# Expert layers of a decay-attention, cosine-MLP and mixture-of-experts kernel: token groups innermost under each half of an expert, and the second layer as seven block products of 256 columns

## The chip, the cores and the metric

The kernel runs on one core of one Trainium2 chip. The metric is the device time of one execution in microseconds (us), lower is better. The engines are TensorE (PE in the rows; PEld is its weight load), VectorE (DVE), ScalarE (ACT), GpSimd (POOL), and SyncE (SP), which issues the transfers.

## What is computed

Three parts follow each other; the output of one is the input of the next.

```python
attn = softmax(causal(scale * q @ k.T + decay(f))) @ v     # 4 x 8 heads, 576 positions, 64 wide
x = attn as [2304 tokens, 512]
h = x @ w_in;  x = (h * cos(h)) @ w_out                     # 512 -> 2048 -> 512
P = exp(x @ w_gate - max); 8 rounds: rows /= their sum, columns /= their sum, *= 2304 / 8
for e in range(8):                                          # the experts: F = 1024
    out += P[:, e:e+1] * (max(x @ w1[e], 0) @ w2[e])        # w1[e] is 512 x 1024, w2[e] 1024 x 512
```

The change lies in the last loop, the experts.

## The kernel before, in words

All matrix products of the experts run in pairs of 16-bit numbers: each fp32 operand is split into a high f16 part (`hi`) and the rest, again in f16 (`lo`), and each product is three passes of TensorE (`PASSES`: hi·hi, hi·lo, lo·hi) that add up in PSUM. Both operands are brought to a common power of two first (`scales`, found by `find_scale` from the largest magnitudes), and `gate` undoes it.

The 2304 tokens are three groups `p` of 768 (two halves of 384), and each expert's F is cut into two halves `hb` of 512. I call the work for one group, one expert and one half of F a **stretch**; there are 3 x 8 x 2 = 48 of them. Before, the loop order is group, expert, half (`blocks`), so the weights of each of the 16 (expert, half) pairs are loaded and prepared three times. Preparing one pair means, per stretch: four transfers of 512 KB into `sg` (`load_raw`, L992), scaling on ACT (`w_scale`, L1045), sums of blocks on POOL for w1 alone (`w1_sums`, L1015, tiles `tm`), the high part on ACT (`w_hi`, L1054) and the low part on POOL in pieces of 256 columns (`w_lo`, L1063, loads the next raw tile at its end).

The **first layer** of a stretch is done in two sets (`m`) of 256 F columns each. A set is a 2 x 2 block product in Winograd's form: seven products of TensorE (`PRODUCTS`, six matmuls of 384 columns each, L1214) instead of eight. Its right-hand operands are seven combinations of the token blocks (`XCS`, tiles `xc`), its left-hand ones seven combinations of weight blocks (`W1T`, tiles `wa`). The seven results are put together by ACT copies (`ct`, L1242) and DVE adds (L1247), then relu and split into the four blocks `h` (`relu_split`, L1231: high part on ACT, low part on DVE). The **second layer** (`second_layer`, L1284) is a plain product: for each of 6 token tiles, 2 sets x 2 z x 3 passes = 12 matmuls of 512 columns (L1291), 72 in a stretch; `leave` (L1302) then adds a token tile, times its gate, into the SBUF accumulator `acc` on DVE (L1320).

Each engine takes its instructions in the order in which the code issues them; nothing reorders them. `hook()` is called after each product and runs the steps of the gate (`sinkhorn`) that are due at that count; `plan` sets after which token tile of the second layer the next stretch's weights are prepared. The seven `xc` tiles of group 0 are made on POOL before the first stretch (`combine_first`, L1083), and those of groups 1 and 2 on DVE and ACT in the last two experts of the group ahead (`combine_sums`, `combine_split`). Just before the experts the MLP part ends (`layer2`, L813, matmuls L822; its results are added into `acc` by DVE, L837).

## Time and profile before

| | |
|---|---|
| time, median of 3 runs | 2078.04 us (2077.55 to 2078.23) |
| profiled execution, first to last instruction (span) | 2075.6 us |
| PE busy | 2049.3 us, 99% of the span |
| ACT, POOL, DVE busy | 1336.1, 1277.9, 1156.3 us (64, 62, 56%) |
| experts, first matmul to last DVE add | 663.13 to 2072.02 us |

How to read it: the profile is of one execution. Its own time is not listed apart from the span; the 2.4 us by which the median of the runs is above the span are what lies around the first and the last instruction. An engine is busy while it computes; matmuls are pipelined, so the mean duration of one matmul in a row (its latency) is longer than its share of the busy time. About two thirds of the span are the experts.

### The profile page before, as it was taken

To read this page: it belongs to the slowest core of one execution; us is meant where nothing else is said; L and a number is where in the kernel's file an instruction comes from. 1 tells how busy PE (TensorE), PEld (TensorE's weight loads), DVE (VectorE), ACT (ScalarE), POOL (GpSimd) and SP (SyncE) were. 2 spreads that over 40 slices of the span, in tenths; PEclk is the share of its full clock that TensorE was granted. 3 is DMA by queue.
4 is the path that set the end of the run, shared out by engine and by line. 5 is a ranking of instruction groups with operands and counts; after the bars stand their busy time and mean duration, and the time that the engine had idled before them with its cause. 6 is when DMAs were issued, how large, how long until landed. Compare 5 with 4: busy or idle time off the path is not lost.

```text
span 2075.6 us, 34054 instructions
## 1 busy us (share of the span) xinstructions
PE 2049.3 (99%) x12461; PEld 1295.1 (62%) x12461; DVE 1156.3 (56%) x2250; ACT 1336.1 (64%) x2479; POOL 1277.9 (62%) x1794
## 2 busy tenths in 40 slices
PE   8999999999999999999999999999999999999999
PEld 6888988898977555555555555555555555555554
DVE  8999788685666654344455444444455444444443
ACT  7888787767654666666566655666566655666553
POOL 7777455151337666766677666766677666766673
PEclk9999999999999999999999999999999999999999
DMA  5454255454301122221222222222222222221221
GB/s 128 101 114 96 71 167 179 127 167 125 109 1 62 51 72 82 72 68 64 82 82 77 87 72 82 73 68 64 82 81 77 87 72 82 72 67 65 82 81 31
DMA packets 176919, 177.52 MB, mean 86 GB/s; under 512 B 64752, under 2 KB 131696, under 8 KB 176752
## 3 DMA queue, kind: packets, MB, share of 16 engines
q1 hardware_dynamic: 176752, 175.35, 27.9%
q8 instruction: 98, 1.61, 0.3%
q14 instruction: 69, 0.57, 0.1%
HBM read 165.54 MB, written 4.87 MB: 82 GB/s over the span
## 4 chain that ended last, share of the span: by engine, by line
PE 91%; DVE 5%; ACT 2%; issue 1%; POOL 1%; DMA 0%; SPq 0%; POOLq 0%; DVEq 0%; ACTq 0%
PE a L1291 36%; PE y L1214 18%; PE bq L1214 13%; PE ph L175 7%; PE a L822 7%; PE pv L593 2%; PE pst L543 2%; PE pss L486 1%; PE pss L487 1%; PE pv L573 1%; PE psq L366 1%; DVE acc L837 1%; POOL w L136 1%; DVE dx L125 1%; DVE t L196 1%
## 5 line engine op out<-in xcount | busy, mean ns | idle before, releaser
L1291 PE MATMUL a<-wb,h 128*128 128x512 f16 x3456 | 754.9, 379 | 0.2 <-ACT acc L1309 0.2
L1291 PEld LDWEIGHTS <-h 128*128 128x128 f16 x3456 | 338.1, 98 | 401.5 <-issue 0.5
L1214 PEld LDWEIGHTS <-wa 128*128 128x128 f16 x4032 | 394.2, 98 | 266.4 <-ACT ct L1242 0.8
L1214 PE MATMUL y<-xc,wa 128*128 128x384 f16 x2304 | 429.5, 326 | 0.1
L1320 DVE SCALAR_TENSOR_TENSOR acc<-a,gate,acc 128x512 f32<-128x512 f32 x264 | 197.3, 749 | 387.9 <-PE a L1291 387.4
L1022 POOL TENSOR_TENSOR tm<-sg 128x256 f32<-128x256 f32 x96 | 71.3, 743 | 447.7 <-issue 429.9
L1214 PE MATMUL bq<-xc,wa 128*128 128x384 f16 x1728 | 327.9, 326 | 0.4 <-ACT ct L1242 0.4
L1242 ACT ACTIVATE ct<-y 128x384 f32<-128x384 f32 x192 | 94.3, 491 | 274.4 <-PE y L1214 274.3
L1072 POOL TENSOR_TENSOR wa<-tm,wa 128x256 f16<-128x256 f32 x384 | 250.3, 686 | 0.0
L1072 POOL TENSOR_TENSOR wb<-sg,wb 128x256 f16<-128x256 f32 x384 | 244.1, 684 | 0.0
L1233 ACT ACTIVATE h<-bq 128x384 f16<-128x384 f32 x288 | 140.8, 489 | 152.3 <-DVE bq L1247 152.1
L1234 DVE SCALAR_TENSOR_TENSOR h<-bq,h 128x384 f16<-128x384 f32 x288 | 159.5, 554 | 127.0 <-ACT h L1233 117.4
L822 PE MATMUL a<-H,w 128*128 128x512 f32 (+1 forms) x960 | 212.6, 369 | 4.9 <-DVE acc L837 2.9
L175 PE MATMUL ph<-xt,w 128*128 128x512 f32 (+1 forms) x960 | 211.5, 369 | 0.0
L1052 ACT ACTIVATE sg<-sg,sw 128x1024 f32<-128x1024 f32 x188 | 209.9, 1142 | 0.0
L822 PEld LDWEIGHTS a<-H,w 128*128 128x128 f32 x960 | 174.4, 188 | 30.3 <-issue 2.5
L1072 POOL TENSOR_TENSOR wa<-sg,wa 128x256 f16<-128x256 f32 x288 | 189.5, 687 | 0.0
L175 PEld LDWEIGHTS ph<-xt,w 128*128 128x128 f32 x960 | 174.9, 188 | 22.8
L1247 DVE SCALAR_TENSOR_TENSOR bq<-bq,ct 128x384 f32<-128x384 f32 x192 | 108.7, 566 | 108.8 <-PE bq L1214 105.1
L1061 ACT CAST wa<-tm 128x1024 f16<-128x1024 f32 x94 | 98.2, 1045 | 97.2 <-POOL tm L1025 97.2
L128 POOL TENSOR_SCALAR w<-dx 128x512 fp32r<-128x512 f32 x32 | 19.8, 620 | 153.9 <-DVE dx L127 149.3
L1061 ACT CAST wb<-sg 128x512 f16<-128x512 f32 x188 | 107.0, 616 | 3.0
(209 smaller groups left out, 2659.4 us busy)
## 6 DMA issues: line engine op xcount, KB each, us to landing
sg<-in_moe_w_dram SPq DMA_DIRECT2D x192, 512.0 KB
seen<-in_moe_w_dram SPq DMA_DIRECT2D x64, 256.0 KB
u<-in_moe_w_dram SPq DMA_DIRECT2D x64, 256.0 KB
stg<-in_moe_w_in_dram SPq DMA_DIRECT2D x16, 512.0 KB
stg<-in_moe_w_out_dram SPq DMA_DIRECT2D x16, 512.0 KB
q<-q SPq DMA_DIRECT2D x30, 160.0 KB
out_dram<-acc SPq DMA_DIRECT2D x18, 256.0 KB
qr<-in_q_dram SPq DMA_DIRECT2D x32, 128.0 KB
```

The lines of the kernel that those rows point to most:

```text
L175: nc.tensor.matmul(ps[:, 0:n], w[:, ws, kk * P : (kk + 1) * P], XT[j][:, xs, kk, :], start=first, stop=kk == KD - 1 and (ws, xs) == PASSES ...
L822: nc.tensor.matmul(a_of[b, j][x][:, 0:n], w[:, s1, DM + x * P : DM + (x + 1) * P], H[:, s2, 0:n], start=i == 0 and n_ == 0, stop=end and n ...
L1052: nc.scalar.activation(t, t, AF.Copy, scale=scale)
L1061: nc.scalar.copy(hi, src)
L1072: nc.gpsimd.tensor_tensor(lo[:, y : y + k, z : z + c], src[:, y : y + k, z : z + c], hi[:, y : y + k, z : z + c], ALU.subtract,)
L1214: nc.tensor.matmul(ps[:, 0:HN], w[:, ws, a, k, :], XCS[p % 2][b][:, xs, k, :], start=fresh and n == 0, stop=n == 5, skip_group_check=not f ...
L1233: nc.scalar.activation(hi, src, AF.Relu)
L1234: lows.append(lambda: nc.vector.scalar_tensor_tensor(lo, src, 0.0, hi, ALU.max, ALU.subtract))
L1242: nc.scalar.activation(c, ps[:, 0:HN], AF.Copy, scale=RAISE)
L1247: nc.vector.scalar_tensor_tensor(c, ps[:, 0:HN], RAISE, other, ALU.mult, ALU.add)
L1291: nc.tensor.matmul(ps, H[:, s1, c * P : (c + 1) * P], W2T[e * NHB + hb & 1][:, 2 * m + z, s2, :], start=start and n == 0, stop=stop and n ...
L1320: nc.vector.scalar_tensor_tensor(a, v, g, a, ALU.mult, ALU.add)
```

## The change

The loop order becomes expert, half, group, and the group order turns round on every other pair (0, 1, 2, then 2, 1, 0). Weights are prepared once for a pair and held for three stretches, in two sets of tiles each for w1 and w2 (`side`). SBUF then holds the `xc` tiles of two groups only: `XB` is group 1's, and `XA` is group 0's and group 2's in turn. These are kept in DRAM (`keep_blocks`) and read back (`fetch_blocks`, seven transfers, 2.75 MB) once in each pair but the first. The tiles of groups 1 and 2 are made in the stretches of the first pair, sums and low parts on POOL (`combine`). Groups 1 and 2 get scales of their own (`x1`, found in the last steps of the MLP, and `x2`), and ACT scales group 1's part of `acc` before the first product of the experts (`scale_group`).

The second layer takes Winograd's form too: per set a 2 x 2 block product over token halves, z and output halves. A stretch has seven products (`PRODUCTS2`) of 2 sets x 3 token tiles x 3 passes = 18 matmuls with 256 columns, 126 matmuls in place of 72. Its left-hand operands are seven blocks `h` per set instead of four (A11, A22 and A12 as before, S1 to S4 new): `kept` makes A11 and A22 (two relus on ACT, low part on POOL), the lines after product 6 and `tails` make the others (DVE and ACT, one low part on POOL). Each list in `tails` is issued after the next product, so those of set 1 are issued in the second layer. Its right-hand operands are seven blocks of w2 (`w_sums` on POOL). Results leave after every product, three DVE instructions of 256 columns (`leave`, `TO` tells which block). PSUM is three banks `y` and five `bq`; three banks `a` are gone. The preparation steps stand in a table by count of `hook` (28 per stretch, 84 per pair): scale, sums, high, low for each of the four weight tiles (`STEADY`, and `FIRST` for the first pair).

```diff
+        second_scale = find_scale("x1", largest[:, 2 * KD : 4 * KD], bank_h)
+        at(after_l1, 79, lambda: next(second_scale))
+        for n in (80, 81):
+            at(after_l2, n, lambda: next(second_scale))
...
+        V11, V21, V22, V1, V2, V3, V4 = range(7)
+        PRODUCTS2 = (
+            ("y", A11, V11), ("b", A12, V21), ("y", S2, V2), ("q", S1, V1), ("y", S3, V3), ("q", S4, V22), ("y", A22, V4),
+        )
...
-        XCS = [blocks_of(0)]
...
-        W1T = [xp.tile([P, 2, 7, 2, P], F16, name=f"wa{m}") for m in range(SETS)]
...
-        W2T = [xp.tile([P, BF, 2, DM], F16, name=f"wb{y}") for y in range(2)]
...
+        def weights_of(kind, y):
+            if kind == "w1":
+                return [xp.tile([P, 2, 7, 2, P], F16, name=f"wa{y}{m}") for m in range(SETS)]
+            return [xp.tile([P, 2, 7, HD], F16, name=f"wb{y}{m}") for m in range(SETS)]
...
+        HT = [[xp.tile([P, 2, HN], F16, name=f"h{m}{c}") for c in range(7)] for m in range(SETS)]
...
+        XD = {g: xd.tile([7, P, 4 * HN], F16, name=f"xd{g}") for g in (0, 2)}
+
+        def blocks_at(p):
+            return XB if p == 1 else XA
+
+        def keep_blocks(p):
+            for c in range(7):
+                nc.sync.dma_start(XD[p][c], XA[c].rearrange("p y k c -> p (y k c)"))
+
+        def fetch_blocks(p):
+            for c in (B11, B21, T2, T1, T3, B22, T4):
+                nc.sync.dma_start(XA[c].rearrange("p y k c -> p (y k c)"), XD[p][c])
...
+        blocks = [(e, hb) for e in range(NE) for hb in range(NHB)]
...
-        blocks = [(p, e, hb) for p in range(NPR) for e in range(NE) for hb in range(NHB)]
...
+                r = stage_of(n).rearrange("p (z d c) -> p z d c", z=2, d=2)
+                tm = tm.rearrange("p (a c) -> p a c", a=4)
+                b11, b12, b21, b22 = r[:, 0, 0], r[:, 0, 1], r[:, 1, 0], r[:, 1, 1]
+                todo = (
+                    (tm[:, 0], b12, b11, ALU.subtract), (tm[:, 2], b12, b22, ALU.subtract),
+                    (tm[:, 1], b22, tm[:, 0], ALU.subtract), (tm[:, 3], b21, tm[:, 1], ALU.subtract),
+                )
+            return [lambda o=o, x=x, y=y, op=op: nc.gpsimd.tensor_tensor(o, x, y, op) for o, x, y, op in todo]
...
+        def scale_group(p, x):
+            a = acc[:, x, p * PAIR : (p + 1) * PAIR]
+            nc.scalar.activation(a, a, AF.Copy, scale=scales[f"x{p}"])
...
+        def bank(kind):
+            return ps_e.tile([P, 512], F32, tag=kind, name=kind, bufs=3 if kind == "y" else 5)
...
-        def relu_split(m, z, h, src):
-            hi, lo = HT[m][z][h][:, 0, :], HT[m][z][h][:, 1, :]
-            nc.scalar.activation(hi, src, AF.Relu)
-            lows.append(lambda: nc.vector.scalar_tensor_tensor(lo, src, 0.0, hi, ALU.max, ALU.subtract))
...
+            def kept(c, ps):
+                r = take("rt", rtmp)
+                nc.scalar.activation(r, cut(ps), AF.Relu)
+                nc.scalar.activation(HT[m][c][:, 0, :], cut(ps), AF.Relu)
+                nc.gpsimd.tensor_tensor(HT[m][c][:, 1, :], r, HT[m][c][:, 0, :], ALU.subtract)
+                return r
...
+            s2 = s2tmp[m]
+            nc.scalar.activation(y, y, AF.Relu, scale=RAISE)
+            nc.vector.scalar_tensor_tensor(b, q, 0.0, r11, ALU.max, ALU.subtract)
+            nc.vector.scalar_tensor_tensor(q, q, 0.0, r22, ALU.max, ALU.add)
+            nc.vector.tensor_tensor(s2, q, r11, ALU.subtract)
+            tails.extend([
+                (lambda: high(A12, y), lambda: high(S2, s2), lambda: low_dve(A12, y), lambda: low_pool(S2, s2)),
+                (lambda: nc.vector.tensor_tensor(c2, y, s2, ALU.subtract), lambda: high(S1, q)),
+                (lambda: high(S3, b), lambda: low_dve(S1, q)),
+                (lambda: high(S4, c2), lambda: low_dve(S3, b)),
+                (lambda: low_dve(S4, c2),),
+            ])
...
-            def part(ps, x, m, start, stop):
-                h, c = divmod(x, HN // P)
-                n = 0
-                for z in range(2):
-                    H = HT[m][z][h]
-                    for s1, s2 in PASSES:
-                        nc.tensor.matmul(
-                            ps,
-                            H[:, s1, c * P : (c + 1) * P],
-                            W2T[e * NHB + hb & 1][:, 2 * m + z, s2, :],
-                            start=start and n == 0,
-                            stop=stop and n == 5,
-                        )
-                        n += 1
...
+                nc.vector.scalar_tensor_tensor(a, v, gate[:, tt, e : e + 1], a, ALU.mult, ALU.add)
...
+            TO = ((0, 0), (0, 0), (0, 1), (1, 1), (1, 1), (0, 1), (1, 0))
+            tail()
+            banks = {}
+            for n, (kind, a, b) in enumerate(PRODUCTS2):
+                fresh = kind not in banks
+                if fresh:
+                    banks[kind] = [bank("y" if kind == "y" else "bq") for _ in range(2)]
+                for m in range(SETS):
+                    for c in range(HC):
+                        ps, at_ = banks[kind][c // 2], c % 2
+                        for z, (s1, s2) in enumerate(PASSES):
+                            nc.tensor.matmul(
+                                ps[:, at_ * HD : (at_ + 1) * HD],
+                                HT[m][a][:, s1, c * P : (c + 1) * P],
+                                W2T[side][m][:, s2, b, :],
+                                start=fresh and m == 0 and at_ == 0 and z == 0,
+                                stop=m == SETS - 1 and z == 2,
+                                skip_group_check=True,
+                            )
+                for c in range(HC):
+                    leave(banks[kind][c // 2], c % 2, c, *TO[n])
+                    if last and n >= 5:
+                        store(c, TO[n][0])
+                tail()
+                hook()
+                hook()
...
+        FIRST = ((44, 47, 53, 56), (46, 52, 70, 72), (50, 63, 73, 78), (75, 79, 82, 85))
+        STEADY = ((17, 18, 23, 26), (22, 32, 45, 47), (48, 54, 73, 75), (50, 58, 76, 82))
...
+        combine_first()
+        keep_blocks(0)
+        prepare_alone(3)
+        for x in range(KD):
+            scale_group(1, x)
...
+        plan_groups()
+        for blk, (e, hb) in enumerate(blocks):
+            side = blk % 2
+            if blk + 1 < len(blocks):
+                plan_weights(blk, STEADY if blk else FIRST)
+            order = (0, 1, 2) if blk % 2 == 0 else (2, 1, 0)
+            for idx, p in enumerate(order):
+                base = blk * NB + idx * NS
+                if (e, hb) == (1, 0):
+                    for x in range(TT):
+                        a = acc[:, :, (p * TT + x) * P : (p * TT + x + 1) * P]
+                        g = gate[:, p * TT + x, 0:1]
+                        put_at(base + 1 + x, lambda a=a, g=g: nc.vector.tensor_scalar(a, a, g, None, ALU.mult))
+                first_layer(side, 0, blocks_at(p))
+                first_layer(side, 1, blocks_at(p))
+                if idx == 0 and blk:
+                    fetch_blocks(order[2])
+                second_layer(side, p, e, hb)
+        assert not plan, plan.keys()
```

On DVE, in any later stretch, the end of the first layer of set 1 and the second layer read as follows before. L1247 are the adds of the seven results, L1234 the low parts of `h`, L1320 the six token tiles that leave.

```order
L1247 SCALAR_TENSOR_TENSOR bq<-bq,ct_8758 128x384
L1234 SCALAR_TENSOR_TENSOR h_8730<-bq,h_8730 128x384
L1247 SCALAR_TENSOR_TENSOR bq<-y,ct_8760 128x384
L1247 SCALAR_TENSOR_TENSOR bq<-bq,ct_8759 128x384
L1234 SCALAR_TENSOR_TENSOR h_8733<-bq,h_8733 128x384
L1234 SCALAR_TENSOR_TENSOR h_8731<-bq,h_8731 128x384
L1234 SCALAR_TENSOR_TENSOR h_8732<-y,h_8732 128x384
L1320 SCALAR_TENSOR_TENSOR acc<-a,gate,acc 128x4x128 x6
```

Now, from the last low part that precedes it (L1313, `h` number 8748 is A12 of set 1; 8750, 8752, 8753 are S1, S3, S4 of set 1; L1364 makes S4):

```order
L1313 TENSOR_TENSOR h_8748<-y,h_8748 128x384
L1389 SCALAR_TENSOR_TENSOR acc<-y,gate,acc 128x2x128 x3
L1364 TENSOR_TENSOR bq<-y,st_8776 128x384
L1389 SCALAR_TENSOR_TENSOR acc<-bq,gate,acc 128x2x128 x3
L1313 TENSOR_TENSOR h_8750<-bq,h_8750 128x384
L1389 SCALAR_TENSOR_TENSOR acc<-y,gate,acc 128x2x128 x3
L1313 TENSOR_TENSOR h_8752<-bq,h_8752 128x384
L1389 SCALAR_TENSOR_TENSOR acc<-bq,gate,acc 128x2x128 x3
L1313 TENSOR_TENSOR h_8753<-bq,h_8753 128x384
L1389 SCALAR_TENSOR_TENSOR acc<-y,gate,acc 128x2x128 x3
L1389 SCALAR_TENSOR_TENSOR acc<-bq,gate,acc 128x2x128 x3
L1389 SCALAR_TENSOR_TENSOR acc<-y,gate,acc 128x2x128 x3
```

Six instructions that leave have become seven groups of three, and four instructions that finish set 1's operands stand between these groups.

On ACT, where the MLP ends and the first product of the experts begins (L201 and L872 belong to the MLP and the gate, L1242 is the copy of the first product's result, L853 splits the last tokens for the gate):

```order
L872 COPY lg<-pl 16x512
L1242 ACTIVATE ct_8724<-y 128x384
L853 CAST xl<-acc 128x512 x2
L1242 ACTIVATE ct_8725<-y 128x384
L1233 ACTIVATE h_8726<-bq 128x384
L853 CAST xl<-acc 128x512
L1242 ACTIVATE ct_8743<-bq 128x384
```

Now four scalings of 768 columns (L1164) stand ahead of the first copy (L1303), and the splits for the gate have moved to later counts:

```order
L872 COPY lg<-pl 16x512
L1164 ACTIVATE acc<-acc,sx_5029 128x768 x4
L1303 ACTIVATE ct_8738<-y 128x384
L1303 ACTIVATE ct_8739<-y 128x384
L1303 ACTIVATE ct_8780<-bq 128x384
L1320 ACTIVATE rt_8754<-bq 128x384
L1321 ACTIVATE h_8740<-bq 128x384
```

On POOL, at the start of the first stretch, the last weight tile was followed by the sums for the next weights (L1022 to L1025; L1050, L1059 and L1072 prepare a weight tile):

```order
L1059 TENSOR_SCALAR wb_8762<-sg_8742 128x512 x2
L1072 TENSOR_TENSOR wb_8762<-sg_8742,wb_8762 128x256 x4
L1022 TENSOR_TENSOR tm_8752<-sg_8750 128x256
L1023 TENSOR_TENSOR tm_8752<-sg_8750 128x256
L1024 TENSOR_TENSOR tm_8752<-tm_8752,sg_8750 128x256
L1025 TENSOR_TENSOR tm_8752<-sg_8750,tm_8752 128x256
L1022 TENSOR_TENSOR tm_8753<-sg_8751 128x256
```

Now (L1120 is the low part of the last weight tile, L1176 the sums for the `xc` tiles of group 1, L1322 and L1316 the low parts of the running stretch's `h`):

```order
L1120 TENSOR_TENSOR wb_8779<-tm_8770,wb_8779 128x256 x4
L1176 TENSOR_TENSOR xs_8783<-acc 128x384
L1176 TENSOR_TENSOR xs_8784<-acc,xs_8783 128x384
L1176 TENSOR_TENSOR xs_8785<-acc 128x384
L1322 TENSOR_TENSOR h_8740<-rt_8754,h_8740 128x384
L1176 TENSOR_TENSOR xs_8786<-acc,xs_8784 128x384
L1176 TENSOR_TENSOR tm_8769<-acc 128x384
L1322 TENSOR_TENSOR h_8742<-rt_8755,h_8742 128x384
L1176 TENSOR_TENSOR tm_8769<-acc,tm_8769 128x384
L1176 TENSOR_TENSOR tm_8770<-acc 128x384
L1316 TENSOR_TENSOR h_8744<-st_8771,h_8744 128x384
```

The low parts that the second layer of the running stretch reads now stand behind sums for group 1 in one queue.

## Rows read from the trace of the kernel before

**Rows 1.** The page, parts 1 and 4: busy time and share; the last chain by engine.

```profile
PE 2049.3 (99%) x12461; PEld 1295.1 (62%) x12461; DVE 1156.3 (56%) x2250; ACT 1336.1 (64%) x2479; POOL 1277.9 (62%) x1794
...
PE 91%; DVE 5%; ACT 2%; issue 1%; POOL 1%; DMA 0%; SPq 0%; POOLq 0%; DVEq 0%; ACTq 0%
```

**Rows 2.** Chain that ended last, by time: start us, us, what.

```profile
1092.42 15.54 PE a L1291 x72
...
1121.61 15.54 PE a L1291 x72
...
2055.69 15.55 PE a L1291 x72
```

**Rows 3.** Windows: length, busy us of each engine (instructions), clock, DMA share, GB/s.

```profile
786.90:816.10 29.20, 29.20 (x158) 15.29 (x157) 12.15 (x20) 17.56 (x30) 19.49 (x32) 1.00 0.22 72
1103.00:1106.00 3.00, 3.00 (x15) 1.37 (x14) 1.81 (x3) 2.97 (x5) 3.00 (x6) 1.00 0.55 171
```

**Rows 4.** Timeline of PE in the attention part: start us, us, instructions.

```profile
151.26 0.78 PE L593 MATMUL pv<-v,A 128*128 128x65 bf16 x20
...
153.59 0.29 PE L486 MATMUL pss<-k,q 128*128 128x256 f32 x1
153.72 0.29 PE L487 MATMUL pss<-k,q 68*128 68x256 f32 x1
153.85 0.63 PE L593 MATMUL pv<-v,A 128*128 128x65 bf16 x15
```

**Rows 5.** Weight loads by form: count | busy us, mean ns of one | idle before.

```profile
L593 PEld LDWEIGHTS <-A 128*128 128x128 f16 x1600 | 55.3, 98 | 11.3 <-ACT ktf L470 3.9 <-DVE A L563 1.1 <-ACT A L555 0.7
```

**Rows 6.** Groups by form, 760 to 2041 us, columns as in rows 5.

```profile
L1320 DVE SCALAR_TENSOR_TENSOR acc<-a,gate,acc 128x512 f32<-128x512 f32 x251 | 187.6, 749 | 369.6 <-PE a L1291 369.3
L1234 DVE SCALAR_TENSOR_TENSOR h<-bq,h 128x384 f16<-128x384 f32 x264 | 146.3, 554 | 118.8 <-ACT h L1233 109.8
...
L1247 DVE SCALAR_TENSOR_TENSOR bq<-bq,ct 128x384 f32<-128x384 f32 x176 | 99.7, 566 | 103.0 <-PE bq L1214 99.2 <-ACT ct L1242 3.7
...
L1242 ACT ACTIVATE ct<-y 128x384 f32<-128x384 f32 x175 | 85.9, 491 | 247.1 <-PE y L1214 247.1
...
L1072 POOL TENSOR_TENSOR wa<-tm,wa 128x256 f16<-128x256 f32 x349 | 227.5, 686 | 0.0
...
L1022 POOL TENSOR_TENSOR tm<-sg 128x256 f32<-128x256 f32 x88 | 65.4, 743 | 408.5 <-issue 408.5
```

**Rows 7.** DVE by form, 240 to 760 us, columns as in rows 5.

```profile
L837 DVE TENSOR_TENSOR acc<-acc,a 128x384 f32<-128x384 f32 x24 | 12.0, 545 | 0.7 <-PE a L822 0.7
...
L609 DVE TENSOR_TENSOR xp<-pv,rc 128x256 f32<-128x256 f32 x1 | 0.4, 423 | 0.0
```

**Rows 8.** Timeline of a first layer (columns as in rows 4; bracket: idle before, releaser).

```profile
1118.52 1.14 PE L1214 MATMUL y<-xc,wa 128*128 128x384 f16 x6
...
1119.50 1.14 PE L1214 MATMUL bq<-xc,wa 128*128 128x384 f16 x6
1119.76 0.57 DVE L1247 SCALAR_TENSOR_TENSOR bq<-y,ct 128x384 f32<-128x384 f32 x1 [0.55 <-PE y L1214]
...
1120.47 1.14 PE L1214 MATMUL y<-xc,wa 128*128 128x384 f16 x6
```

**Rows 9.** Timeline where the experts begin.

```profile
640.55 0.92 POOL L1091 TENSOR_TENSOR xc<-tm,xc 128x384 f16<-128x384 f32 x1
643.03 1.02 POOL L1094 TENSOR_TENSOR tm<-acc,tm 128x384 f32<-128x384 f32 x1
...
661.27 2.74 DVE L837 TENSOR_TENSOR acc<-acc,a 128x512 f32<-128x512 f32 x4 [0.70 <-PE a L822]
662.73 2.57 POOL L1072 TENSOR_TENSOR wb<-sg,wb 128x256 f16<-128x256 f32 x4
663.13 1.15 PE L1214 MATMUL y<-xc,wa 128*128 128x384 f16 x6
...
728.33 1.14 PE L1214 MATMUL y<-xc,wa 128*128 128x384 f16 x6
```

**Rows 10.** Line L913: duration ns min/median/max, first and last start, form.

```profile
L913 ACT ACTIVATE acc<-acc,sx x4: 924/933/945, 616.8 to 625.8; 128x768 f32<-128x768 f32 x4
```

**Rows 11.** Timeline of the end.

```profile
2071.27 0.75 DVE L1320 SCALAR_TENSOR_TENSOR acc<-a,gate,acc 128x512 f32<-128x512 f32 x1 [1.84 <-PE a L1291]
```

## What was predicted, before the changed kernel had run

> **What bounds the kernel now.** I read the page first. TensorE is busy for 99% of the span and holds 91% of the last chain; the other three engines are at 56 to 64% [rows 1]. So what counts is TensorE's time, and whether the others can still hand it its operands in time.
>
> The chain by time shows the second layer as one unbroken piece of 15.54 us that comes back every 29.19 us (1121.61 - 1092.42), up to the last at 2055.69 [rows 2]. From this the price of a matmul: 15.54 / 72 = 215.8 ns with 512 columns, and (29.19 - 15.54) / 84 = 162.5 ns with 384 in the first layer. The 128 columns between them cost 53.3 ns, so a matmul costs 2.5 ns beside its columns, in both layers. In one stretch TensorE is full at granted clock 1.00, while DVE works 12.15, ACT 17.56 and POOL 19.49 of 29.20 us, and transfers move 72 GB/s [rows 3]. The experts run from 663.13; the first two stretches end at 728.33, 65.2 us for 2 x 29.19 = 58.4: the gate's steps cost 6.8 us there [rows 9]. The change keeps these steps, so I leave them in.
>
> **What the second layer costs on TensorE.** 72 matmuls of 512 columns go, 126 of 256 come: 7/8 of the columns, 7/4 of the matmuls and weight loads. No 256-column f16 matmul is in the trace. Extended along the two known lengths it costs 162.5 - 53.3 = 109.2 ns, and the layer 126 x 109.2 = 13.76 us, 1.78 less per stretch, 85.5 in 48. The bounds: without the 2.5 ns it is 106.7 ns (13.44 us, 101 less). From above, the nearest rows are matmuls with 256 columns of fp32 in the attention part, which start 0.13 us apart [rows 4]: 16.38 us, 0.84 more, 40 us more in all. What speaks for the low end is the weight load. One shows 98 ns [rows 5], which would only just lie beside 109 ns; but 20 pairs of load and matmul with 64 or 65 columns take 0.78 us, and 15 take 0.63, so each further pair takes 0.03 us [rows 4]. The loads are f16 and 128x128 there, as here. They follow each other at 31 ns and do not set a pace of 109. I take 109.2.
>
> **Do the others keep up?** A stretch is now 27.41 us. Per set DVE has three adds, three sums, one difference for S4 and four low parts: 22 instructions per stretch at 0.56 us [rows 6], 12.3 us. 21 instructions bring the results out. Their length is not in the trace: half of 749 ns would be 375, the one DVE row of 256 columns with a PSUM operand shows 423, and 566 at 384 columns is a safe top; three-operand adds are 10 to 20 ns above two-operand ones at 384 (554 or 566 against 545) [rows 6, 7]. I take 450: 9.5 us, 21.8 in all. ACT has 26 instructions of 0.49 = 12.7, and the preparation: 17.56 - 16 x 0.49 = 9.7 us before, at most 7/4 of that for w2's seven blocks, but once in three stretches: 5.7 [rows 3, 6]. POOL has 6 low parts of 0.92 [rows 9], and a third of four tiles of 4 x 0.74 + 7 x 0.69 us [rows 6]: 5.5 + 10.4. So DVE 80%, ACT 67%, POOL 58%: none is the bound over a stretch.
>
> What matters is the order within it. In the first layer, the add after product 4 starts 0.26 us after it (the six matmuls end where the next six start) and ends at 1120.33, 0.14 before product 6 begins, which writes the same bank [rows 8]. That margin stays if DVE is free by then. In set 1 the low parts of set 0 stand ahead of this add (each waits for an ACT copy of 0.49); added up, the last of them ends 4.9 us after the set begins, the add can start at 5.1. Then product 5's add and three sums end 1.8 us after the first layer (T + 1.8), the low part of A12 at T + 2.4. TensorE reads it in product 1 for set 1 at T + 1.97 + 0.98 + 0.2 = T + 3.1. From there, each product of 1.97 us leaves DVE 3 x 0.45 + 0.55 = 1.9 us of work, so it neither falls behind nor catches up. A bank is written again two products later, when its first two parts have been out for 0.7 us, and the low parts of S1, S3 and S4 come 0.9 us before set 1 reads them. So nothing waits: 0 us, covered by margins of 0.2 (before product 6 of the first layer) and 0.7 (second layer). POOL's low part of A11 has 1.5 us, and its other work is spread by the table.
>
> Transfers: a pair now moves 2.1 MB of weights and 2.75 MB of token tiles in 82 us, 59 GB/s against 72 before and 171 where they run densely [rows 3]. The fetch may start when the first stretch's first layer ends, and is needed 41 us later; at 171 GB/s it takes 16. On SP's queue only the load of the fourth weight tile stands close behind it, and that has 16 us more. Hidden: 0.
>
> **What is added once.** First, the start. The scale of group 1 is computed on DVE behind the four last adds of the MLP, which end at 664.0 [rows 9]. Three tiny instructions (some 0.5 us, an estimate) and four scalings of 0.93 [rows 10] later it is 668.2, and the copy behind them on ACT ends at 668.7. Product 2 waits for that copy, since it adds to the same bank; TensorE would be there at 665.4 (663.13, some 0.3 for the scale's own steps, two products). I take 3.3 us; 0 at the least, 5 if the preparation of the gate is also late.
>
> Second, POOL in the first pair. Before the first stretch it ends its last weight tile at 665.3 [rows 9]; the w2 tile with sums ends about 666. In stretch 1 it then has 8 sums of 1.02, 14 low parts and 6 of `h` at 0.92 [rows 9], 26.6 us in one queue. The low part of A11, set 1, stands behind 8 sums and 5 low parts, some of which wait for TensorE; I get 683.3, where TensorE wants it at 681.6 or so: 1.7 us. S2 costs the same again. Stretch 2 has 26.6 + 5.9 us for 27.4: another 1.3, and stretch 3 some 0.8 until the queue is empty. 5.5 us; between 0 and 15, if POOL's whole surplus is waited for.
>
> Third, the end. Before, 3.6 us lie between the last add (2072.02) and the end at 2075.6 [rows 11]; now three stores end together instead of one, 0.26 MB or 1.5 us each at 171 GB/s [rows 3], partly over each other, after a shorter add: +1, at most +3.
>
> **Sum.** -85.5 + 3.3 + 5.5 + 1 = -75.7. The profiled span 2075.6 becomes 1999.9; with the 2.4 us by which the median of the runs lies above it, 2002.3.
>
> **Rivals.**
> (A) The short matmul does not hide its weight load. For it speaks that the load's 98 ns leave 11 ns, and the fp32 rows at 0.13 us; against it the 31 ns per pair. At 0.13 it is +40 + 10 = 2128, slower. It decides from (15.54 - 9.8 / 48) / 126 = 121.7 ns a matmul. 5%. By the same mechanism the Trainium skill ("TensorE: Matmul & The Clock Gate", Back-to-back issue gap) gives pairs of load and matmul 81 ns at 128 columns, 25 more than the matmul alone; an estimate from that page with 25 ns on top of 109 is 16.9 us a layer and about 2153 us in all. The trace disagrees with that section at both ends: 215.8 ns at 512 columns, where it has 131, and 31 ns at 64.
>
> (B) DVE cannot bring the results out in time. At 566 ns each a product leaves it 2.25 us of work in 1.97; six times 0.28 less the margin of 0.7 is 1 us per stretch, 48 in all: 2050. For it: 749 at 512 is more than two-operand rows suggest, perhaps due to `acc`'s strides; against: 423 at 256. It begins near 0.5 us. 12%.
>
> (C) The first pair, or POOL's and ACT's queues in the later ones, cost more than added up: every wait above sits in one queue, and 16 pairs repeat it. 10 to 25 us more: 2012 to 2027. 14%.
>
> (D) None of the added waits arise: 1992. 5%.
>
> **How the numbers follow.** The forecast, 1996 to 2011, has 64%; A 5, B 12, C 14, D 5. The range from 1994 to 2030 leaves out A, most of B and part of D. Faster by over 0.2% (4 us, about what a measurement of this kernel can tell from no change): everything but A, 0.94; the same 0.01; slower 0.05.
>
> **What would show it.** Right: second layers of 13.76 us in the chain, 27.41 from one to the next; DVE's groups of three at about 0.45 us each; ACT's scalings before a first wait of about 3 us at 666; waits on POOL's low parts in the first pair alone; no wait for the fetched tiles. Wrong: 256-column matmuls more than 110 ns apart, a wait of TensorE on `acc` or on a low part in every stretch, or one on a transfer in each pair.

## The result, and the profile after

| | before | changed |
|---|---|---|
| median of the runs, us | 2077.98 (2077.55 to 2078.23) | 2017.74 (2016.69 to 2018.17) |
| profiled span, us | 2075.6 | 2016.5 |
| experts' first matmul to the end of the span, us | 1412.5 | 1352.0 |

The ratio is 0.9709, 95% interval 0.9695 to 0.9723: faster by 60 us. The forecast's sum was 2002.3; the time lies 15.4 us above it, inside the range from 1994 to 2030 but outside the likeliest case's own 1996 to 2011, among the times of rival C.

The page of the changed kernel, parts 1 and 4, answers to [rows 1]: TensorE's share is lower although the kernel is faster, and DVE stands in the last chain with 9% where it had 5%.

```profile
PE 1970.5 (98%) x15056; PEld 1550.4 (77%) x15056; DVE 1508.1 (75%) x3316; ACT 1217.3 (60%) x2557; POOL 1098.0 (54%) x1392
PE 82%; DVE 9%; ACT 4%; POOL 2%; issue 2%; DMA 1%; SPq 0%; POOLq 0%; DVEq 0%; ACTq 0%
```

The chain by time in the middle answers to [rows 2] (start us, us, what). The second layer is seven pieces of 1.97; the first one starts at 1201.54, the last at 1213.33, and the next stretch's at 1228.94: 27.40 from one to the next.

```profile
1201.54 1.97 PE y L1408 x18
...
1213.33 1.97 PE y L1408 x18
...
1228.94 1.97 PE y L1408 x18
```

The windows of the experts, one for each of the first six stretches (from a stretch's first matmul to the next one's), then the 42 others, the end, and three stretches of the middle for [rows 3] (columns as there):

```profile
664.48:708.00 43.52, 33.04 (x214) 22.71 (x215) 30.71 (x54) 26.12 (x55) 30.64 (x35) 0.84 0.04 13
708.00:743.84 35.84, 33.16 (x245) 24.39 (x243) 19.61 (x47) 27.20 (x60) 25.78 (x31) 1.00 0.20 78
743.84:773.65 29.81, 28.14 (x215) 21.02 (x215) 21.57 (x54) 18.46 (x42) 26.02 (x38) 1.00 0.18 55
...
860.00:2009.88 1149.88, 1149.88 (x8813) 862.08 (x8811) 849.96 (x1822) 620.50 (x1300) 606.90 (x826) 1.00 0.18 60
2009.88:2016.50 6.62, 0.16 (x2) 0.00 (x0) 1.14 (x3) 0.00 (x0) 0.00 (x0) 0.78 0.80 222
...
1200.00:1282.20 82.20, 82.20 (x632) 61.63 (x631) 60.10 (x130) 45.12 (x95) 45.23 (x62) 1.00 0.19 60
```

From 860 us on TensorE is never idle: the steady stretches are as forecast. What is missing from the gain lies almost all in the first 200 us of the experts. The first stretch takes 43.52 in place of 27.41, the second 35.84, the third 29.81, and the mean granted clock of the first is 0.84.

TensorE's waits from 664 us on (engine, line, what it waited for: us in total, times, longest):

```profile
PE bq L1408 <- DVE acc L1386: 7.2, 1, 7.2
PE y L1287 <- DVE bq L1307: 3.3, 3, 1.2
PE bq L1408 <- DVE h L1313: 2.4, 1, 2.4
PE y L1287 <- ACT ct L1303: 2.3, 2, 2.0
PE bq L1287 <- DVE cf L1256: 1.8, 4, 0.5
```

The longest, 7.2 us for a DVE leave, is followed by time order (timeline: start us, us, engine, instruction, idle before and releaser):

```profile
687.63 8.92 DVE L1235 TENSOR_TENSOR xl<-acc,xl 128x512 fp32r<-128x512 f32 x1 [1.77 <-ACT xl L1234]
688.12 0.93 POOL L1316 TENSOR_TENSOR h<-st,h 128x384 f16<-128x384 f32 x1
688.98 0.94 POOL L1191 TENSOR_TENSOR xc<-xs,xc 128x384 f16<-128x384 f32 x1
689.86 0.93 POOL L1191 TENSOR_TENSOR xc<-tm,xc 128x384 f16<-128x384 f32 x1
...
695.07 0.94 POOL L1191 TENSOR_TENSOR xc<-tm,xc 128x384 f16<-128x384 f32 x1
696.48 1.07 DVE L1386 TENSOR_TENSOR acc<-acc,bq 128x256 f32<-128x256 f32 x3
697.27 1.46 PE L1408 MATMUL bq<-wb,h 128*128 128x256 f16 x6 [7.23 <-DVE acc L1386]
```

L1235 is the low part of one stripe of the tokens for the gate, one DVE instruction with two inputs and the output in SBUF. Three of the four take 0.67 to 0.73 us; this one is "busy" for 8.92. In the kernel before, the same four instructions (L854 there, between 665.35 and 670.55) took 0.68 us each; POOL ran nothing beside them, since it was idle from 665.30 to 682.89.

```profile
L854 DVE TENSOR_TENSOR xl<-acc,xl 128x512 fp32r<-128x512 f32 x4 | 2.7, 684 | 1.3 <-ACT xl L853 1.3
```

The long one ends at 696.55, half a microsecond after POOL's run of instructions without a gap ends (696.0). Behind it in DVE's queue stand the leaves that TensorE waits for. After the wait the granted clock is 0.50 (1.2 GHz) for 4.02 us and 0.72 for 2.78, so two products that take 1.97 each elsewhere cost 2.9 more. Wait and clock make 10.1 us. The window of the first of these products:

```profile
697.27:701.29 4.02, 4.02 (x19) 2.84 (x20) 3.33 (x9) 1.44 (x3) 1.00 (x1) 0.50 0.00 0
```

**Theory 1:** DVE is shut out of this instruction as long as POOL's instructions, which read SBUF too, follow each other without a gap. **Theory 2:** DVE and POOL simply have too much to do in the first stretches, and the work is late wherever it stands.

### The profile page after: what moved, and what is told of

The parts are those of the page before. It is cut to its first block, busy times and chain, and to the rows that moved or that the text cites. A ratio compares the mean times of both kernels' runs of the same rounds, so it can differ in the third digit from the quotient of the medians.

```text
span 2016.5 us, 40078 instructions
## 1 busy us (share of the span) xinstructions
PE 1970.5 (98%) x15056; PEld 1550.4 (77%) x15056; DVE 1508.1 (75%) x3316; ACT 1217.3 (60%) x2557; POOL 1098.0 (54%) x1392
## 4 chain that ended last, share of the span: by engine, by line
PE 82%; DVE 9%; ACT 4%; POOL 2%; issue 2%; DMA 1%; SPq 0%; POOLq 0%; DVEq 0%; ACTq 0%
PE y L1408 18%; PE y L1287 18%; PE bq L1408 14%; PE bq L1287 13%; PE ph L175 4%; PE a L822 4%; PE pv L593 2%; PE pst L543 2%; PE pss L486 1%; PE pss L487 1%; PE pv L573 1%; DVE t L196 1%; POOL w L136 1%; DVE dm L135 1%; PE psq L366 1%
## 5 line engine op out<-in xcount | busy, mean ns | idle before, releaser
L1408 PEld LDWEIGHTS <-h 128*128 128x128 f16 x6048 | 592.9, 98 | 85.8 <-DVE acc L1386 7.5
L1322 POOL TENSOR_TENSOR h<-rt,h 128x384 f16<-128x384 f32 x192 | 175.8, 915 | 466.1 <-ACT h L1321 459.0
L1408 PE MATMUL y<-wb,h 128*128 128x256 f16 x3456 | 409.7, 273 | 0.5 <-POOL h L1316 0.5
L1303 ACT ACTIVATE ct<-y 128x384 f32<-128x384 f32 x192 | 94.3, 491 | 426.4 <-PE y L1287 426.2
L1408 PE MATMUL bq<-wb,h 128*128 128x256 f16 x2592 | 308.6, 274 | 9.6 <-DVE acc L1386 7.2
L1389 DVE SCALAR_TENSOR_TENSOR acc<-y,gate,acc 128x256 f32<-128x256 f32 x504 | 212.5, 477 | 48.8 <-PE y L1408 48.8
L1389 DVE SCALAR_TENSOR_TENSOR acc<-bq,gate,acc 128x256 f32<-128x256 f32 x378 | 159.6, 477 | 39.4 <-PE bq L1408 39.2
L1307 DVE SCALAR_TENSOR_TENSOR bq<-bq,ct 128x384 f32<-128x384 f32 x192 | 107.6, 560 | 76.5 <-PE bq L1287 69.9
L1313 DVE TENSOR_TENSOR h<-bq,h 128x384 f16<-128x384 f32 x288 | 157.6, 549 | 2.6
L1307 DVE SCALAR_TENSOR_TENSOR bq<-y,ct 128x384 f32<-128x384 f32 x96 | 54.3, 565 | 125.9 <-PE y L1287 123.5
L1310 ACT CAST h<-bq 128x384 f16<-128x384 f32 x288 | 134.6, 483 | 14.1 <-DVE bq L1364 14.0
L1316 POOL TENSOR_TENSOR h<-st,h 128x384 f16<-128x384 f32 x96 | 88.1, 918 | 87.2 <-ACT h L1310 84.8
L1320 ACT ACTIVATE rt<-bq 128x384 f32<-128x384 f32 x192 | 93.7, 488 | 24.6 <-DVE bq L1307 22.5
```

The lines of the kernel that those rows point to most:

```text
L1303: nc.scalar.activation(c, cut(ps), AF.Copy, scale=RAISE)
L1307: nc.vector.scalar_tensor_tensor(cut(c), cut(ps), RAISE, other, ALU.mult, ALU.add)
L1310: nc.scalar.copy(HT[m][c][:, 0, :], src)
L1313: nc.vector.tensor_tensor(HT[m][c][:, 1, :], src, HT[m][c][:, 0, :], ALU.subtract)
L1320: nc.scalar.activation(r, cut(ps), AF.Relu)
L1322: nc.gpsimd.tensor_tensor(HT[m][c][:, 1, :], r, HT[m][c][:, 0, :], ALU.subtract)
```

## The experiments

All of them change the changed kernel. Profiled executions of one kernel are not alike to the microsecond before the experts begin, so the last two columns count from the experts' first matmul. Even these are not free of chance. Behind the wait of 2.0 us at the start (ACT's `ct`, 666.6 to 668.6 in the changed kernel) the granted clock was 0.55 for the next 3.82 us:

```profile
668.58:672.40 3.82, 3.82 (x14) 1.90 (x15) 2.32 (x4) 0.49 (x1) 0.83 (x1) 0.55 0.02 4
```

It was 0.57 and 0.60 in e11_control and e9_psum, but 1.00 in e1_memset, e2_spread, e4_end, e5_copy, e6_gate and e7_margin, which have the same wait and the same two products ahead of it. In the changed kernel that is worth 1.9 us. The edits of these kernels take effect later than this place, so they are not behind it; what is stays open. e7_margin, which only adds work, stands 2.4 us below the changed kernel in the last column, while its median is 0.4 us lower. So a difference of 2 us in that column shows nothing by itself.

| kernel | median, us | ratio to before (95%) | first matmul | to the end of the span |
|---|---|---|---|---|
| changed | 2017.74 | 0.9709 (0.9695 to 0.9723) | 664.48 | 1352.0 |
| e1_memset | 2009.85 | 0.9679 (0.9660 to 0.9697) | 664.70 | 1341.9 |
| e2_spread | 2015.57 | 0.9701 (0.9685 to 0.9717) | 664.41 | 1348.5 |
| e5_copy | 2011.39 | 0.9681 (0.9667 to 0.9695) | 665.27 | 1344.0 |
| e9_psum | 2013.07 | 0.9688 (0.9674 to 0.9703) | 665.40 | 1345.8 |
| e11_control | 2012.79 | 0.9686 (0.9670 to 0.9703) | 664.83 | 1346.0 |
| e3_scale_later | 2015.68 | 0.9699 (0.9685 to 0.9714) | 665.46 | 1348.6 |
| e4_end | 2014.11 | 0.9696 (0.9682 to 0.9711) | 665.60 | 1346.9 |
| e6_gate | 2011.64 | 0.9682 (0.9668 to 0.9696) | 664.12 | 1345.0 |
| e7_margin | 2017.33 | 0.9710 (0.9695 to 0.9724) | 664.96 | 1349.6 |
| e8_all | 2008.44 | 0.9669 (0.9652 to 0.9685) | 664.40 | 1342.4 |
| e10_best | 2001.00 | 0.9628 (0.9614 to 0.9643) | 664.97 | 1332.3 |
| e12_bank | 1998.33 | 0.9617 (0.9604 to 0.9630) | 664.41 | 1331.3 |

**e1_memset: more work on POOL.**

```diff
...
                 put_at(14 + n - 6, lo_[n])
+                put_at(14 + n - 6, lambda: nc.gpsimd.memset(gap0[:, 0:1], 0.0))
```

> Adds work: after each of the last eight low parts that POOL makes for group 1 (slots 14 to 21 of the first stretch) POOL also clears one column of an unused tile, which writes SBUF but reads nothing. Theory 1 (DVE's difference of two SBUF tiles on L1235, 8.92 us in the changed kernel, is shut out as long as POOL's reads of SBUF follow each other without a gap): the small writes let it in, it takes under 2.5 us, TensorE's wait of 7.2 us on the leaves falls under 1.5 us and the slow matmuls after it (2.9 us) go too: 2007 to 2010 us. Theory 2 (DVE and POOL simply have too much to do in this stretch): more work on POOL cannot help; L1235 stays at 8 to 9.5 us and the time is 2017 to 2019. Theory 1 in a stricter form (only an empty queue on POOL lets DVE in): also 2017 to 2019, and then the next kernel of this group decides.

Its timeline (columns as above):

```profile
686.17 2.85 DVE L1235 TENSOR_TENSOR xl<-acc,xl 128x512 fp32r<-128x512 f32 x1 [1.77 <-ACT xl L1234]
687.56 0.92 POOL L1191 TENSOR_TENSOR xc<-xs,xc 128x384 f16<-128x384 f32 x1
688.41 0.10 POOL L1441 MEMSET gap<- 128x1 f32 x1
688.46 1.33 POOL L1191 TENSOR_TENSOR xc<-tm,xc 128x384 f16<-128x384 f32 x1
```

DVE comes in right at the first memset, and POOL's next instruction is 0.41 us longer. TensorE's wait falls from 7.2 to 1.1 us and the clock stays at 1.00 behind it: 9.0 us less (6.1 of wait, 2.9 of clock), by work that was added. (The last column has 10.1 us less, since the clock at the start was 1.00 as well.) Theory 2 falls for this wait; the strict form (only an empty queue lets DVE in) falls too. But one of the four runs took 2017.54 us, as long as the changed kernel, and the profiled one is the fastest (2008.36): that the memset lets DVE in every time is not shown.

**e5_copy: the instruction in between reads SBUF.**

```diff
...
+                put_at(14 + n - 6, lambda: nc.gpsimd.tensor_copy(gap0[:, 0:1], scales["x0"]))
```

> As e1_memset, but the small instruction on POOL between the low parts copies one column from another tile: it reads SBUF too. If what let DVE in was that the instruction between does not read SBUF (theory 1 in the form: DVE's two-input operation is shut out while POOL reads follow each other): L1235 stays near 9 us and the time is 2017 to 2019. If any change of instruction on POOL, or its short start, lets DVE in: L1235 takes under 3.5 us and the time is 2008 to 2011, as with the memset.

L1235 takes 2.84 us, TensorE waits 1.1 for the leave: as with the memset; the median, 2011.39, lies just above the expected 2008 to 2011. So what lets DVE in is not that the instruction between leaves SBUF unread; that part of theory 1 was wrong.

**e2_spread: POOL's slots apart.**

```diff
-            for n in range(6, 14):
-                put_at(14 + n - 6, highs[n])
-                put_at(14 + n - 6, lo_[n])
+            for n, s in enumerate((14, 16, 18, 19, 21, 22, 24, 25), 6):
+                put_at(s, highs[n])
+                put_at(s, lo_[n])
```

> The same eight low parts of group 1 and the copies ahead of them stand at slots 14, 16, 18, 19, 21, 22, 24 and 25 in place of 14 to 21; nothing else changes. Theory 1: POOL waits for its next slot several times between 684 and 696 us, the L1235 operations take 0.7 to 2 us each, TensorE's wait of 7.2 us and the 2.9 us of slow matmuls go: 2006 to 2010. Theory 2: DVE's work is the same and as late; 2016 to 2019.

L1235 took 7.20 us (685.88 to 693.08), TensorE waited 5.5. The expectation missed: POOL was behind its slots, so spreading them only ended its run earlier, at 692.54. DVE again came out half a microsecond after the run's end, which fits theory 1; the time would fit theory 2 as well.

**e9_psum and e11_control: one input from PSUM, everything else alike.**

```diff
                 nc.scalar.copy(XL[:, 0, x, :], a)
-                nc.vector.tensor_tensor(XL[:, 1, x, :], a, f32(XL[:, 0, x, :]), ALU.subtract)
+                ps = spare()
+                nc.scalar.copy(ps[:, 0:n], a)
+                nc.vector.tensor_tensor(XL[:, 1, x, :], ps[:, 0:n], f32(XL[:, 0, x, :]), ALU.subtract)
```

The control has the two added lines, but keeps `a` as DVE's input.

> ACT copies each of the four stripes for the gate a second time, to a free PSUM bank, and DVE's difference on L1235 (L1237 here) takes that copy as its first input in place of the SBUF stripe. DVE's instruction has the same size and place, POOL's stream beside it is the same, ACT has 4 x 0.65 us more. Theory 1 (DVE's instruction with two inputs in SBUF is shut out by POOL's reads that follow without a gap; with one input in PSUM it is not): it takes 0.7 to 0.8 us each time, TensorE's wait of 7.2 us falls under 1 us, the slow products behind it go: 2006 to 2009 us. If any use of SBUF by DVE beside POOL's stream were shut out: it stays near 9 us and the time at 2016 to 2019.

> The control for e9_psum: ACT makes the same second copy to PSUM, but DVE still takes both inputs from SBUF (the copy in PSUM is not used). Theory 1: L1237 takes 7 to 10 us once, as in the changed kernel, and the time is 2016 to 2019. If e9_psum gains by the later place that the added copy gives to DVE's instruction, this one gains the same: under 2011.

Timeline of e9_psum:

```profile
688.61 0.91 POOL L1318 TENSOR_TENSOR h<-st,h 128x384 f16<-128x384 f32 x1
689.05 0.69 DVE L1237 TENSOR_TENSOR xl<-bq,xl 128x512 fp32r<-128x512 f32 x1 [2.26 <-ACT bq L1236]
689.48 0.91 POOL L1191 TENSOR_TENSOR xc<-xs,xc 128x384 f16<-128x384 f32 x1
689.79 1.86 PE L1410 MATMUL bq<-wb,h 128*128 128x256 f16 x12 [2.78 <-DVE xl L1237]
```

Timeline of e11_control:

```profile
687.99 5.16 DVE L1237 TENSOR_TENSOR xl<-acc,xl 128x512 fp32r<-128x512 f32 x1 [1.77 <-ACT xl L1234]
...
691.69 0.91 POOL L1191 TENSOR_TENSOR xc<-tm,xc 128x384 f16<-128x384 f32 x1
...
695.00 0.92 POOL L1191 TENSOR_TENSOR xc<-xs,xc 128x384 f16<-128x384 f32 x1 [2.41 <-ACT xc L1188]
```

The instruction itself decides it: with one input in PSUM 0.69 us in the midst of POOL's run (all four 0.68 to 0.69); with both in SBUF 5.16, until that run ends at 692.6. The Trainium skill ("SBUF — State Buffer", Who interferes with whom, and Summary: rules for kernel authors) states that a DVE instruction with two SBUF inputs contends with a GpSimd instruction that reads SBUF, and that the second to issue is blocked until the first has finished. The traces agree on who contends. On the length the measurement decides: DVE was held not through one POOL instruction but through nine in a row.

Both times missed what was expected (2006 to 2009, and 2016 to 2019). By the last column the control gained 6 us by itself: the added copies hold up ACT, POOL waits 2.4 us for it, and that gap ends DVE's wait after 5.16 us. And e9_psum lost what it gained: the PSUM bank that it borrows is the next one that the second product takes (e12_bank below tests this), so TensorE waits 2.8 us for L1237, and the granted clock behind that is 0.81 for 1.5 us and 0.57 for the next product (3.15 us). So these two times do not tell the theories apart; the lengths of the instruction do, and e10_best below shows the gain.

**e3_scale_later: the start.**

```diff
-        for x in range(KD):
-            scale_group(1, x)
...
+            for n, x in enumerate((0, 2, 1, 3)):
+                put_at(n, lambda x=x: scale_group(1, x))
...
-                put_at(n, fn)
+                put_at(n + (n < 4), fn)
```

> The four scalings of group 1 on ACT leave the place ahead of the first stretch and stand at its slots 0 to 3; POOL's first four sums come one slot later. Theory 1: the copy after the first product is no longer behind 3.4 us of scalings, so TensorE's wait of 2.0 us at 668.6 goes, and with it the slow matmuls behind it (1.9 us), and POOL's wait of 4.35 us for the first layer's results; the 8.92 us of L1235 may become shorter or not, since POOL's stream behind it moves: 2013 to 2015 if it stays, 2004 to 2007 if it goes. Theory 2 (the first stretch is bound by the sum of its work, wherever it stands): the time comes back later in the stretch, 2016 to 2018.

The wait of 2.0 us at 668.6 is gone (0.3 is left of ACT's `ct`), so it came from the scalings. But TensorE waits 1.5 for POOL's low parts in place of 0.5, L1235 takes 9.71, and all waits together fall by 1.0 us only (18.9 to 17.9). The rest of the 3.4 us in the last column is clock: 1.9 at the start, which six kernels that keep the wait don't have either, and 0.8 in the second product behind the long wait. The median, 2015.68, lies between the ranges of the two theories (2013 to 2015, 2016 to 2018): what the scalings' place is worth in the end is not shown.

**e4_end: the last stores.**

```diff
...
-                    out[tt * P : (tt + 1) * P, :].rearrange("t (k c) -> t k c", k=KD), acc[:, :, tt * P : (tt + 1) * P]
+                    out[tt * P : (tt + 1) * P, :].rearrange("t (k c) -> t k c", k=KD)[:, 2 * d : 2 * d + 2],
+                    acc[:, 2 * d : 2 * d + 2, tt * P : (tt + 1) * P],
...
-                    if last and n >= 5:
-                        store(c, TO[n][0])
+                    if last and n in (1, 4, 5, 6):
+                        store(c, *TO[n])
```

> In the last stretch each half of a token tile's columns is stored as soon as it is complete (after products 2, 5, 6 and 7), so that the last product leaves three stores of 64 KB x 2 instead of six transfers of whole rows in its neighbourhood. If the end of the changed kernel (6.6 us from TensorE's end to the span's end, 4.55 before) comes from the bytes that are stored last: 1 to 2 us less, 2016 of the runs' median and 5 us from TensorE's end to the span's end. If it comes from the fixed time of a store: 0 to 0.3 us less.

The last leaves start 4.5 us before the end (2007.99 of 2012.5); in the changed kernel it is 6.75 (2009.75 of 2016.5). Behind the last product three stores follow in both kernels, of half as many bytes each here, so the bytes cost 2.2 us. The other 2.9 us of the difference in the table come from the part before. TensorE's waits are the same there (18.9 us in both), but the two products behind the long wait took 3.62 and 1.97 us in place of 4.02 and 2.78, and the clock at the start was 1.00 (1.9 us).

**e6_gate: the gate's steps.**

```diff
             nc.scalar.activation(gate, gate, AF.Exp, bias=small["ngm"])
+            yield
             rows()
...
+                yield
                 if it + 1 < 8:
                     rows()
...
-        for n, x in enumerate((0, 1, 2, 3, 5, 7, 9, 15, 18, 21, 24, 29, 32, 35, 39, 57, 64, 85, 92, 113, 120, 141, 148)):
+        for n, x in enumerate((0, 1, 2, 3, 5, 7, 9, 15, 18, 21, 24, 29, 32, 35, 50, 52, 57, 58, 78, 80, 85, 86, 106, 108, 113, 114,
+                           134, 136, 141, 142, 162, 164)):
```

> The gate's steps alone are moved: the row sums no longer follow the Exp in the same step but one step later, both go to the end of the second stretch's second layer (slots 50 and 52 in place of 39), and each of the eight iterations is cut in two parts, one iteration in the first products of a stretch's first layer, one behind its fifth and sixth product of the second layer (before: slots 1 and 8 of a stretch's first layer). Theory 1 (the 8.3 us that TensorE waits from 728 us on, 2.4 for a low part behind the row sums, 3.3 for adds and 1.8 for the gate's sums in set 1, are DVE's queue with the gate's steps in the wrong places): 5 to 8 us less, 2010 to 2013. Theory 2 (in the first six stretches DVE is short of time whatever the order): the waits move to other products, 2016 to 2018.

As theory 1 has it, the waits on L1307, on L1313 at 728 and on `cf` are gone, and the median of 2011.64 lies in its range. One wait of 2.0 for the column sums is new, so the waits fall from 18.9 to 13.1, by 5.8 us. (The 7.0 us less in the last column hold the 1.9 of clock at the start too, and are diminished by a granted clock of 0.62 behind the new wait, from 740.97 to 745.50.) The new wait is the shut-out again, in the row sums just ahead (timeline of e6_gate): a 128x18 TENSOR_SCALAR, 0.18 to 0.25 us elsewhere, beside POOL's low parts and sums of weights.

```profile
735.53 0.29 DVE L1213 TENSOR_REDUCE rs<-gate 128x18 f32<-128x144 f32 x1
735.86 3.44 DVE L1214 TENSOR_SCALAR rs<-rs 128x18 f32<-128x18 f32 x1
739.33 0.27 DVE L1215 RECIPROCAL rs<-rs 128x18 f32<-128x18 f32 x1
```

**e7_margin: how near is rival B?**

```diff
                 nc.vector.scalar_tensor_tensor(a, v, gate[:, tt, e : e + 1], a, ALU.mult, ALU.add)
+                nc.vector.tensor_scalar(gap0[:, 0:1], v[:, 0, 0:1], 1.0, None, ALU.mult)
```

> Adds work: behind each leave of the experts after the first DVE also copies one column of the same bank, 21 short instructions a stretch, 0.15 us each as other 128x1 instructions show. It asks how far the steady stretch is from the prediction's rival B. In the trace three leaves take 1.27 us, a low part 0.46, and DVE idles 0.23 us a product where low parts come and 0.70 in the last three. By the prediction's steps: 0.45 more a product is 0.2 too much in four products, 0.9 us in a row, against a margin of 0.7: 0.2 to 0.5 us of waiting a stretch, 8 to 21 us in 42 stretches, 2026 to 2039. If the margin (the banks' turn) is larger than that: 2017 to 2020. If each leave's bank is waited for directly: 0.45 x 7 a stretch, over 2100.

No wait arises (windows of three stretches):

```profile
1199.86:1282.06 82.20, 82.20 (x632) 61.64 (x630) 63.86 (x193) 45.19 (x95) 45.20 (x63) 1.00 0.18 59
```

The test was weaker than meant: 63 instructions add 3.76 us of DVE's time, 0.06 each, since they overlap their neighbours. A leave with its companion takes 0.46 us from start to start (0.40 without), three of them and a low part just fill a product. So rival B begins above 0.46 us a leave, from start to start; where exactly was not tried. The median, 2017.33, is the changed kernel's within 0.4 us, as the expectation's case of a larger margin has it.

**e8_all, e10_best, e12_bank: together.** e8_all is e1_memset, e3_scale_later, e4_end and e6_gate. e10_best has e9_psum's copy in place of the memset, and the Exp and its row sums at slots 37 and 39. e12_bank moves the borrowing steps:

```diff
-        for n, x in enumerate((0, 1, 2, 3, 5, 7, 9, 15, 18, 21, 24, 29, 32, 35, 37, 39, 57, 58, 78, 80, 85, 86, 106, 108, 113, 114,
+        for n, x in enumerate((0, 1, 2, 3, 5, 7, 9, 16, 20, 22, 24, 29, 32, 35, 37, 39, 57, 58, 78, 80, 85, 86, 106, 108, 113, 114,
```

> e1_memset, e3_scale_later, e4_end and e6_gate together. If each repairs a wait of its own, the differences add up: from first matmul of the experts to the end of the span 1352.0 in the changed kernel, less 10.1, 3.4, 2.2 (the end alone) and 5 to 8: 1329 to 1332, that is 1995 to 1998 us. If they share one cause (a stretch that is full), it stays near e1_memset: 2005 to 2009.

> e9_psum with e3_scale_later, e4_end and the gate's steps as in e6_gate, but the Exp at slot 37 and its row sums at 39 (there both waits of e6_gate's row sums, 2.0 us, should shrink to about 1). Each cause by itself, counted from the first matmul of the experts to the end of the span (1352.0 in the changed kernel): 10 for the shut-out, 3.4 for the start, 2.2 for the end, 7 for the gate: 1329, that is 1994 to 1998 us of the runs' median, against 2008.4 of e8_all, in which the shut-out came back. If the 10 us are lost again in another place: 2004 to 2008.

> e10_best with the four steps of the gate that borrow a PSUM bank moved from slots 15, 18, 21 and 24 to 16, 20, 22 and 24, so that none of them stands right ahead of the product that takes two new banks (the second and fourth of the second layer). If TensorE's wait of 2.6 us at 686 in e10_best (on L1237, in the middle of the second product) is that the product's second bank is the one just borrowed: the wait goes, 2 to 3 us less from the first matmul of the experts to the end of the span (1332.3 in e10_best): 1329 to 1330.5, 1997 to 1999.5 us of the runs' median. If DVE's instruction itself is late there, the wait moves to the next product and the time stays at 2000 to 2002.

e8_all missed its sum by more than 10 us. Its median of 2008.44 is among the times expected if all share one cause, but its trace says otherwise: the shut-out is back, memsets and all.

```profile
684.18 9.97 DVE L1235 TENSOR_TENSOR xl<-acc,xl 128x512 fp32r<-128x512 f32 x1 [2.16 <-ACT xl L1234]
687.17 0.12 POOL L1447 MEMSET gap<- 128x1 f32 x1
687.23 0.94 POOL L1191 TENSOR_TENSOR xc<-tm,xc 128x384 f16<-128x384 f32 x1
...
693.51 0.13 POOL L1447 MEMSET gap<- 128x1 f32 x1
```

Seven memsets passed without letting DVE in, where in e1_memset the first did. With the input in PSUM (e10_best) all four take 0.68 to 0.69 us, the long wait and the slow clock behind it stay away, and the last column is 10.1 us below e8_all's (some of that from the row sums' new place). It missed the expected 1329 and 1994 to 1998 with 1332.3 and 2001.00: 2.6 us of TensorE's wait for the borrowed bank were left, and the 7 us that the expectation counts for the gate hold the clock at the start, which its 3.4 us have already. In e12_bank that wait is gone as expected, but one of 1.1 for POOL's low part (L1320) has come, so the last column shows 1.0 less (2 to 3 were expected) and the medians 2.7; the two kernels' intervals overlap. The waits of e12_bank:

```profile
PE bq L1413 <- DVE h L1317: 1.5, 1, 1.5
PE bq L1291 <- DVE h L1317: 1.5, 2, 0.8
PE y L1413 <- POOL h L1320: 1.1, 1, 1.1
```

Its clock is 1.00 over the first stretch. It beats both kernels: 0.9617 of the kernel before, interval 0.9604 to 0.9630, and 1998.33 / 2017.74 = 0.990 of the changed one.

## Why the prediction was right, and where it was wrong

**The second layer: right.** From 1201.54 to the end of the last piece (1213.33 + 1.97) it is 13.76 us for 126 matmuls, 109.2 ns each, as forecast. Rival A is out, by the 12.5 ns that are left to its 121.7. The stretch is 27.40, forecast 27.41.

**The others keep up: right in the steady part.** No wait after 860 us. Three leaves take 1.27 us where 3 x 0.45 = 1.35 was put; DVE is at 73% (80 forecast), POOL and ACT at 55% (58 and 67). The fetched tiles are never waited for.

**What is added once: mis-sized.** Forecast 3.3 + 5.5 + 1 = 9.8 us; the profile has 26.6, and these 16.8 us more are the miss (a span of 2016.5 where 1999.9 was forecast):
- *The start*, 3.3: the first matmul is 1.35 late, the wait 2.0, and 1.9 more went at a granted clock of 0.55 behind it (668.58 to 672.40): 5.3. The wait's mechanism is right. That 1.35 + 2.0 hits 3.3 is in part luck, since 0.3 and 3.0 were forecast. The 1.9 of clock were not in the sum, and six other executions with the same wait don't have them.
- *POOL in the first pair*, 5.5: its own low parts cost 0.5. The queue's backlog was real, but it struck through DVE: 10.1 us of shut-out and slow clock, a mechanism that the prediction did not have. POOL's run without a gap is the change's own: it moves the token groups' sums and low parts to POOL, and stands them beside the gate's stripes on DVE.
- *The gate's steps*, taken as paid ("the change keeps these steps, so I leave them in"): this step failed. Before, TensorE waited 0.8 us in all in the experts; now the same steps stand in a DVE queue of 43 instructions a stretch (130 in three) where it had 20 [rows 3], and 8.6 us of waits come up around them (3.3, 2.4, 1.8, and 0.8 and 0.3 of small ones). e6_gate shows it for most of that: the waits fall by 5.8 us by moving the steps alone, and the median by 6.1. TensorE's waits in the experts before:

```profile
PE bq L1214 <- ACT ct L1242: 0.4, 1, 0.4
PE a L1291 <- ACT acc L1309: 0.2, 1, 0.2
PE bq L1179 <- DVE cs L1153: 0.2, 1, 0.2
```

- *The end*, 1: it is 2.1 (6.6 against 4.5 from TensorE's end to the span's), and e4_end shows that the bytes stored last make it.

5.3 + 0.5 + 10.1 + 8.6 + 2.1 = 26.6, and -85.5 + 26.6 = -58.9, against 2016.5 - 2075.6 = -59.1.

Rival C's price was right (2012 to 2027), its words half: every one of these waits sits in one queue, but none repeats in 16 pairs, and POOL's and ACT's queues made less of them than DVE's. Rival D (1992, no added waits) is not far from e12_bank, which has 5.4 us of waits left.

## What to carry to other kernels

Price a change in the steady state by the nearest lengths, and then walk through the first pass of each loop by itself: there one-off work stands in queues that the change has tightened, and work "kept" isn't free. A long instruction in a trace may be a long wait: look at what runs without a gap beside it, and test by moving one operand, not by moving the work. A wait of some microseconds can be paid twice, by the clock behind it, and not in every execution: before a microsecond or two of a profile is put down to an edit, look whether the clock at an untouched place is the same in both.

## What the runs showed of the hardware

- A DVE instruction whose inputs both lie in SBUF was held through up to 9.97 us of POOL instructions in a row; so was a 128x18 TENSOR_SCALAR with one SBUF input (3.44 us in e6_gate, where its other seven took 0.18). Why that one was held stays open. DVE instructions with an input in PSUM ran beside the same stream at their usual length. Whether a short POOL instruction lets DVE in varies (e1_memset at the first, e8_all at none of seven); on what it depends stays open.
- TensorE's granted clock was 1.00 behind waits of 1.1 us (e1_memset) and 2.39 us (728.30 to 730.69, changed kernel), but 0.50 (1.2 GHz) for 4.02 us behind one of 7.2. Behind the same wait of 2.0 us at the start, with the same two products ahead, it was 0.55 to 0.60 over 3.82 us in three executions and 1.00 in six: what tells these apart stays open.
- Small DVE instructions behind others cost 0.06 us from start to start, though the profile gives each 0.15.
